# State products with stationary operands of 48 columns, the state added in two parts of 48 rows

## The chip, the cores and the metric

The kernel runs on one core of a Trainium2 chip. The core has five engines with a queue each: TensorE (PE in the profile; PEld is its loading of the stationary operand), VectorE (DVE), ScalarE (ACT), GpSimd (POOL) and SyncE (SP, which issues DMAs here). The metric is the device time of one execution in microseconds, the median of several runs. All arithmetic is fp32; on TensorE each product of fp32 operands shows as two passes, so each is two loads and two multiplications in the counts.

## What is computed

A linear attention with a state (the delta rule) over 4 batches, 8 heads, 768 steps and 48 columns per head, followed by a two-layer network with an exact GELU over the 3072 resulting rows:

```python
for t in range(S):                                   # S = 768, D = 48
    kt, vt, bt = k_n[:, :, t], v[:, :, t], beta[:, :, t, None]     # k_n: k over its norm
    y[:, :, t] = np.einsum('bhd,bhde->bhe', q[:, :, t], state)
    v_old = np.einsum('bhde,bhd->bhe', state, kt)
    state = state + bt[:, :, :, None] * np.einsum('bhd,bhe->bhde', kt, vt - v_old)
x = y.transpose(0, 2, 1, 3).reshape(B * S, H * D)    # 3072 x 384
h = x @ w_in                                         # 384 x 2048
out = (0.5 * h * (1.0 + erf(h / sqrt(2)))) @ w_out   # 2048 x 384
```

The state of each batch and head is a matrix of 48 x 48.

## The kernel before

The 768 steps are cut into NC = 12 chunks of C = 64. A unit is one chunk of a pair of batches (NA = 2 units per chunk, u.a = 0 and 1), so a unit's 128 rows are 64 steps of two batches. p (0 or 1) is the batch within the pair. The eight heads are written h = 2 j + r with j in 0..3 and r in 0 or 1.

Within a chunk the recurrence is solved at once: Gram matrices of the keys (`grams`, L368), an elimination on VectorE over 32 x 32 blocks (`eliminate_steps`, L443 and L445), two joins of blocks (`join_run`, L518), and then per chunk `state_steps`:

- `against_state` multiplies keys and queries with the state (L573) and forms W (L581, L582);
- `solve` makes U = Z W (L598), copied by ScalarE (L604);
- `outputs` calls `use` for both units: per unit 16 products with P, the masked query-key matrix (L616), into psY, and then `update`, 16 products of keys and U (L625), into psS. psY and psS are parts of one tile over two PSUM banks, hence both show as psY in the profile. For each unit there follow on VectorE `next_state` (L630), which adds psS to the state, and `read` (L639), four additions that make x, one row of the network's input per step;
- `turn` transposes x on TensorE (L660) into psX, and ScalarE copies it to xT (L661).

The state is a tile of 128 rows by unit, p, j and 48 columns: the rows of r = 0 begin at row 0, those of r = 1 at row 64. A head's state fills 48 of its 64 rows; in Kp, which holds the keys, the columns 48 to 63 of each head are zero (a memset at the start), and so rows 48 to 63 and 112 to 127 of psS and of the state are zero. Nothing reads those rows but the addition itself: `against_state` takes rows r * 64 to r * 64 + 47.

The network runs one chunk behind the attention: in stage c + 1 the chunk c goes through the first layer, 16 blocks of three products (`fc1`, L678) with a GELU on ScalarE (L680), and the second layer. From chunk 2 on the second layer is done in seven products of blocks in place of eight (`two`, L716), in the order n = 1, 5, 2, 6, 4, 7, 3. Products 6 and 7 use the same columns of the tile Y: 6 writes Y[:, 0], VectorE reads it (`read2`, L758), and 7 adds onto it (start is not set), is read by L761, and so on to L769. `mix` (L725 to L730) makes sums of G for these products on VectorE.

The order of work comes from `emit`, which sorts all steps by a time in units of stages. In the loop of stages only VectorE keeps the order in which the steps are emitted (`manual_schedule` with DVE alone); for the other engines a planner, which simulates the program with estimated costs, chooses the order within each queue. Chunk 0 and the start are emitted before the loop, in an order fixed for all engines, with `update` and `next_state` called for chunk 0 on their own. `update` and `next_state` are called for chunks 0 to 10: chunk 11 needs no further state.

"Stage w" below is the stretch in which state_steps(w) runs. In the profile the bursts of L625 begin at 58.0 us (chunk 0), 90.3 (1), 172.4 (2), 216.1 (3), 272.1 (4), 317.4 (5), 373.1 (6), 418.4 (7), 474.1 (8), 519.4 (9) and 572.8 (10).

Of the kernel before, what the change touches and what calls it, by code (L numbers as in the profile page):

```python
# [11 lines left out]
ALU = mybir.AluOpType  # L12
# [4 lines left out]
def kernel(  # L17
# [28 lines left out]
    nc = tc.nc  # L46
    B, H, S, D = q.shape
    DM, DF = moe_w_in.shape
    C = 64
# [8 lines left out]
    HALF = [slice(0, C), slice(C, 2 * C)]  # L58
# [40 lines left out]
    for c in range(NC):  # L99
        for a in range(NA):  # L100
            u = tiles[c, a] = Unit()
# [77 lines left out]
    St = cpool.tile([128, NA, 2, NP, D], F32)  # L179
# [426 lines left out]
    def use(us):  # L606

        for u in us:
            psY = dn("psY")
            u.psY = quarters(psY[:, :, 0:NP * D])  # L610
            u.psS = psY[:, :, NP * D:2 * NP * D].rearrange("q p (j d) -> q p j d", d=D)
            for k in range(NP // 2):
                for r in range(2):
                    for p, s in SIDES:
                        h = 4 * k + 2 * s + r
                        nc.tensor.matmul(u.psY[HALF[p ^ s], p, k, r, :], lhsT=u.P[HALF[p], h, :],  # L616
                                         rhs=u.U[HALF[p], h, :], start=True, stop=True)
            if u.c > 0:
                update(u)

    def update(u):
        if u.c < NC - 1:
            for j in range(NP):
                for r, p in QUADS:
                    nc.tensor.matmul(u.psS[HALF[r], p, j, :], lhsT=u.Kp[HALF[p], 2 * j + r, :],  # L625
                                     rhs=u.U[HALF[p], 2 * j + r, :], start=True, stop=True)

    def next_state(u):
        if u.c < NC - 1:
            nc.vector.tensor_tensor(St[:, u.a], St[:, u.a], u.psS, op=ALU.add)  # L630

    def read(u, copy=nc.scalar.copy):
        u.x = wk.tile([128, H, D], F32, tag="x", name="x")
# [7 lines left out]
    def outputs(us):  # L641
        use(us)
        for u in us:
            next_state(u)
            read(u)
# [252 lines left out]
    for u in first[:NA]:  # L898
        update(u)
# [4 lines left out]
    for u in first[:NA]:  # L904
        next_state(u)
# [44 lines left out]
    for w in range(3, NC):  # L950
# [6 lines left out]
        if w % 2:  # L957
            plan += [at(w + 0.09, w + 0.092, gram + query), at(w + 0.25, w + 0.95, state_steps(w))]
            if two_ahead:
                rows = eliminate_steps(w // 2 + 1)  # L960
# [45 lines left out]
```

## Time and profile before

| | us |
|---|---|
| median of 9 runs | 675.86 |
| lowest and highest | 674.47, 676.84 |
| the profiled execution | 675.02 |
| its span, first to last instruction | 673.3 |
| PE, DVE, ACT, POOL busy | 643.7, 452.3, 229.1, 82.1 |
| L625, 704 multiplications, busy | 14.9, 226 ns each |
| L625, 704 loads, busy | 13.1, 143 ns each |
| L630, 22 instructions, each (median) | 0.554 |
| L639, 80 instructions, each (median) | 0.356 |

Busy time of an engine counts overlapping instructions once. Small products on different quadrants of the array overlap, so their durations say little of the rate: what counts is the distance between starts. The mean granted TensorE clock is 0.98. In lines of the order of time the columns are start, duration of the merged group, engine, line, operation, written tile and read tiles, shape and count; in brackets stands how long the engine had been idle and what ended that.

### The profile page before, as it was taken

How to read it: one execution, taken by the hardware profiler on the slowest of the kernel's cores; microseconds unless marked ns; L12 is line 12 of the kernel's file. 1: busy time of each engine (PE TensorE's matmuls, PEld its weight loads, DVE VectorE, ACT ScalarE, POOL GpSimd, SP SyncE). 2: the span in 40 equal slices, each digit the busy share in tenths (PEclk: the TensorE clock that was granted, in tenths of full speed). 3: DMA queues.
4: the chain of work that ended last, by engine and by line, in shares of the span. 5: the costliest groups of instructions: out<-in, count | busy, mean ns of one | idle time of the engine just before them, and what ended most of it. 6: DMA issues, size and time to landing. Idle time of an engine off the chain costs nothing.

```text
span 673.3 us, 21703 instructions
## 1 busy us (share of the span) xinstructions
PE 643.7 (96%) x9542; PEld 561.4 (83%) x9542; DVE 452.3 (67%) x921; ACT 229.1 (34%) x605; POOL 82.1 (12%) x82
## 2 busy tenths in 40 slices
PE   6868998899899999999999999999999999999997
PEld 5666775676689989989989989989989989989996
DVE  6999999994689846479846479846479844324021
ACT  3457754614342143142143142143142132132220
POOL 4050300113111021111021111020111010000000
PEclk9966999999999999999999999999999999999999
DMA  8886565203432233511342511211301210100101
GB/s 124 187 245 171 114 177 130 47 1 65 84 45 34 52 46 51 82 31 27 57 53 44 85 27 27 52 21 31 67 3 26 55 17 3 25 1 2 24 1 25
DMA packets 158271, 39.76 MB, mean 59 GB/s; under 512 B 149984, under 2 KB 153056, under 8 KB 158176
## 3 DMA queue, kind: packets, MB, share of 16 engines
q1 hardware_dynamic: 152224, 33.26, 26.3%
q10 hardware_dynamic: 5952, 5.12, 3.3%
q8 instruction: 75, 1.23, 0.8%
q14 instruction: 20, 0.16, 0.1%
HBM read 33.62 MB, written 4.72 MB: 57 GB/s over the span
## 4 chain that ended last, share of the span: by engine, by line
PE 82%; DVE 10%; ACT 3%; issue 2%; DMA 2%; ACTq 0%; SPq 0%; DVEq 0%
PE psH L678 35%; PE psY L716 12%; PE psX L716 12%; PE psZ L716 4%; PE psK L573 3%; PE psJ L518 3%; PE psG L368 3%; PE psO L691 3%; PE psU L598 2%; PE psY L616 2%; DVE Nu L445 2%; DVE tmp L443 2%; DVE w_e L235 1%; DMA Kp<-in_k_dram 1%; PE psY L625 1%
## 5 line engine op out<-in xcount | busy, mean ns | idle before, releaser
L678 PE MATMUL psH<-xT,w_in_sb 128*128 128x256 f32 x1152 | 262.6, 384 | 4.1 <-ACT o_sb L695 2.3
L678 PEld LDWEIGHTS psH<-xT,w_in_sb 128*128 128x128 f32 x1152 | 216.0, 191 | 35.9 <-ACT o_sb L695 3.0
L680 ACT ACTIVATE G<-psH 128x256 f32<-128x256 f32 x192 | 73.6, 384 | 183.6 <-PE psH L678 171.6
L445 DVE TENSOR_TENSOR Nu<-Nu,tmp 128x30 f32<-128x30 f32 (+9 forms) x180 | 62.8, 349 | 6.2
L443 DVE TENSOR_TENSOR tmp<-Nu 128x30 f32<-128x30 f32 (+9 forms) x180 | 60.0, 333 | 5.1
L716 PE MATMUL psY<-w_out_sb,G 128*128 128x192 f32 x320 | 57.1, 330 | 1.1 <-DVE u L761 0.5
L716 PE MATMUL psX<-w_out_sb,G 128*128 128x192 f32 x320 | 56.2, 329 | 0.0
L716 PEld LDWEIGHTS psY<-w_out_sb,G 128*128 128x128 f32 x320 | 51.6, 190 | 3.1 <-DVE u L761 2.5
L716 PEld LDWEIGHTS psX<-w_out_sb,G 128*128 128x128 f32 x320 | 52.2, 190 | 0.7
L691 PE MATMUL psO<-w_out_sb,G 128*128 128x384 f32 x128 | 45.1, 495 | 1.6 <-DVE w_out_sb L236 1.6
L661 ACT COPY xT<-psX 128x384 f32<-128x384 f32 x24 | 11.4, 478 | 103.1 <-PE psX L660 102.0
L306 POOL TENSOR_TENSOR n<-n,half 128x16 f32<-128x16 f32 x10 | 29.4, 2939 | 88.8 <-DVE n L281 67.7
L691 PEld LDWEIGHTS psO<-w_out_sb,G 128*128 128x128 f32 x128 | 23.1, 190 | 16.9 <-DVE w_out_sb L236 4.0
L604 ACT COPY U<-psU 64x192 f32<-64x192 f32 x96 | 30.1, 313 | 19.6 <-PE psU L598 18.3
L403 DVE TENSOR_TENSOR P<-psG,mask 128x1024 f32<-128x1024 f32 x10 | 12.2, 1225 | 35.8 <-PE psG L368 35.8
L581 DVE TENSOR_TENSOR W<-psK,V 128x384 f32<-128x384 f32 x22 | 12.1, 551 | 29.1 <-ACT y L580 29.0
L725 DVE TENSOR_TENSOR S<-G 128x512 f32<-128x512 f32 x20 | 14.3, 714 | 25.8 <-ACT G L680 25.8
L467 POOL MEMSET Zf<- 32x512 f32 x23 | 12.4, 540 | 153.2 <-DVE Zf L458 152.2
L333 POOL TENSOR_TENSOR V<-V,n 128x384 f32<-128x384 f32 x18 | 17.1, 953 | 106.3 <-DMA V<-in_v_dram 57.7
L639 DVE TENSOR_TENSOR x<-psY,y 64x192 f32<-64x192 f32 x80 | 28.3, 354 | 0.9
L526 DVE TENSOR_TENSOR XM<-psJ,gm 32x512 f32<-32x512 f32 x20 | 13.8, 690 | 22.0 <-PE psJ L518 21.8
L716 PE MATMUL psY<-T,G 128*128 128x192 f32 x160 | 28.2, 329 | 0.0
(135 smaller groups left out, 878.4 us busy)
## 6 DMA issues: line engine op xcount, KB each, us to landing
Kp<-in_k_dram SPq DMA_DIRECT2D x76, 96.0 KB, 3.4
w_out_sb<-in_moe_w_in_dram SPq DMA_DIRECT2D x24, 256.0 KB, 4.2
V<-in_v_dram SPq DMA_DIRECT2D x48, 96.0 KB, 3.1
out_dram<-o_sb ACTq DMA_DIRECT2D x48, 96.0 KB, 2.2
w_raw<-in_moe_w_out_dram SPq DMA_DIRECT2D x10, 384.0 KB, 4.6
Zf<-in_moe_w_out_dram SPq DMA_DIRECT2D x6, 384.0 KB, 4.7
Qp<-in_q_dram SPq DMA_DIRECT2D x64, 32.0 KB, 2.2
Qp<-in_q_dram SPq DMA_DIRECT2D x16, 96.0 KB, 4.2
```

The source lines that it names most:

```text
L306: nc.gpsimd.tensor_tensor(flat, flat, half, op=ALU.pow)
L368: nc.tensor.matmul(psG[HALF[p], r, i * NP + j, :], lhsT=u.Kt[rows, p, j, :], rhs=(u.Qt if x else u.Kt)[rows, p, j, :], start=True, stop=True)
L443: nc.vector.tensor_tensor(tmp, nu[:, j + 1:, j:j + 1].to_broadcast([128, n, j]), nu[:, j:j + 1, 0:j].to_broadcast([128, n, j]), op=ALU.mult)
L445: nc.vector.tensor_tensor(nu[:, j + 1:, 0:j], nu[:, j + 1:, 0:j], tmp, op=ALU.add)
L518: nc.tensor.matmul(psJ[to, i, :], lhsT=(xm if level else off)[rows, u, :], rhs=zf[rows, u, HB:C] if level else xm[rows, u, :], start=True, ...
L573: nc.tensor.matmul(u.psK[to, x, r, j, :], lhsT=(u.Qt if x else u.Kt)[rows, p, j, :], rhs=St[rows, u.a, p, j, :], start=True, stop=True)
L604: copy(pairs(u.U[HALF[p]], s), u.psU[HALF[p ^ s], p])
L639: nc.vector.tensor_tensor(dst, src, pairs(u.y[HALF[p ^ s]], s), op=ALU.add)
L678: nc.tensor.matmul(psH, lhsT=w_in_sb[:, f // 2, m, f % 2 * 128:(f % 2 + 1) * 128], rhs=xTs[c][:, m, :], start=(m == 0), stop=(m == NM - 1))
L680: nc.scalar.activation(G[:, f, :], psH, ACT.Gelu)
L691: nc.tensor.matmul(u.psO, lhsT=G[:, f, u.a * 128:(u.a + 1) * 128], rhs=w_out_sb[:, f, :], start=(f == 0), stop=(f == NF - 1))
L716: nc.tensor.matmul(ps_, lhsT=lhs[:, f, :], rhs=rhs[:, f, :], start=first and f == 0, stop=f == FH - 1, skip_group_check=not first)
```

## The change

For chunks 2 to 10 the products of `update` take only the first 48 columns of each head's keys as the stationary operand, in place of 64 with the zero columns, and so write 48 rows of psS per r. The rows 48 to 63 and 112 to 127 of psS are then not written in those chunks, and `next_state` adds in two instructions, rows 0 to 47 and rows 64 to 111. Chunks 0 and 1 stay as they were.

```diff
@@ -622,12 +622,15 @@
         if u.c < NC - 1:
             for j in range(NP):
                 for r, p in QUADS:
-                    nc.tensor.matmul(u.psS[HALF[r], p, j, :], lhsT=u.Kp[HALF[p], 2 * j + r, :],
+                    m = C if u.c < 2 else D
+                    nc.tensor.matmul(u.psS[r * C:r * C + m, p, j, :],
+                                     lhsT=u.Kp[HALF[p], 2 * j + r, 0:m],
                                      rhs=u.U[HALF[p], 2 * j + r, :], start=True, stop=True)
 
     def next_state(u):
         if u.c < NC - 1:
-            nc.vector.tensor_tensor(St[:, u.a], St[:, u.a], u.psS, op=ALU.add)
+            for rows in [slice(0, 128)] if u.c < 2 else [slice(r * C, r * C + D) for r in range(2)]:
+                nc.vector.tensor_tensor(St[rows, u.a], St[rows, u.a], u.psS[rows], op=ALU.add)
```

## The prediction

> **What bounds the kernel now.** I read the page's first lines, then the table of stretches, then the order of time around the changed lines. The page:
>
> ```profile
> span 673.3 us, 21703 instructions
> ...
> PE 643.7 (96%) x9542; PEld 561.4 (83%) x9542; DVE 452.3 (67%) x921; ACT 229.1 (34%) x605; POOL 82.1 (12%) x82
> ...
> PE 82%; DVE 10%; ACT 3%; issue 2%; DMA 2%; ACTq 0%; SPq 0%; DVEq 0%
> ```
>
> TensorE (PE) is busy for 96% of the span and holds 82% of the chain that ended last. The table of stretches over two stages of the middle (stretch, its length, then the busy time of each engine) says how hard the bound is there:
>
> ```profile
> 260.00:310.00 50.00, 50.00 (x733) 45.62 (x732) 35.38 (x79) 15.78 (x40) 8.66 (x6) 1.00 0.35 57
> 310.00:361.00 51.00, 50.88 (x851) 46.08 (x850) 34.06 (x72) 15.37 (x37) 4.97 (x5) 1.00 0.26 41
> ```
>
> PE has no gap in them at a granted clock of 1.00, while VectorE (DVE) is busy for 34 to 35 of some 50 us. So time taken off PE's queue shortens these stages, and time put on DVE costs only where PE stands waiting for it. The question is how much room DVE has just behind the state sum. The order of time of stage 5 (start, us, engine, line, tiles, count):
>
> ```profile
> 318.31 0.56 PEld L625 LDWEIGHTS psY<-U,Kp 64*64 64x64 f32 x32
> ...
> 319.14 0.55 DVE L630 TENSOR_TENSOR St<-St,psY 128x384 f32<-128x384 f32 x1
> 319.61 1.45 DVE L639 TENSOR_TENSOR x<-psY,y 64x192 f32<-64x192 f32 x4
> 321.09 0.55 DVE L630 TENSOR_TENSOR St<-St,psY 128x384 f32<-128x384 f32 x1
> ...
> 321.56 1.46 DVE L639 TENSOR_TENSOR x<-psY,y 64x192 f32<-64x192 f32 x4
> ...
> 323.05 0.36 DVE L758 TENSOR_TENSOR u<-psY,p 128x192 f32<-128x192 f32 x1
> ...
> 324.08 0.41 PEld L660 LDWEIGHTS psX<-ident,x 128*128 128x128 f32 x3
> ...
> 324.46 2.58 PEld L716 LDWEIGHTS psY<-w_out_sb,G 128*128 128x128 f32 x16
> ```
>
> DVE works through sum, read, sum, read, L758 in one piece. The product at 324.46 (n = 7) adds onto the psY columns that L758 reads, so it may not begin before L758 is done, at 323.41: 1.05 us of room. Stages 7 and 9 repeat this to 0.01 us. Stage 3 has none left:
>
> ```profile
> 223.01 0.36 DVE L758 TENSOR_TENSOR u<-psY,p 128x192 f32<-128x192 f32 x1
> ...
> 223.42 2.57 PEld L716 LDWEIGHTS psY<-w_out_sb,G 128*128 128x128 f32 x16 [0.26 <-DVE u L758]
> ```
>
> There PE already stands 0.26 us for L758, and starts 0.05 us after its end (223.37).
>
> **What the change adds and removes.** It touches c = 2 to 10 with two units each: 18 bursts of L625 (of 22) and 18 sums of L630. No wait, tile, DMA or order by hand is changed.
>
> *PE.* A burst has 16 products in two passes, 32 pairs of load and multiplication. From the starts of the single records they come in groups of four quadrants, one group per 58 ns, so 8 x 58 = 0.465 us, which is also the distance from the burst before (L616 at 317.85) to the one at 318.31 above. What sets the 58? L368 streams 64 columns over a 64-column operand, L573 and L625 stream 48 over 64: all three take 58. So the streamed width does not decide up to 64, and the stationary width may. The trace has no operand of 48 columns. Bounds: 58 ns (L625 itself) and 33 ns per group of four, of L419, whose operands have 32 columns (and stream 32). Linear between them 48 gives 45.5, which I take: 12.5 x 8 = 0.10 us less per burst, 0.20 per stage, 18 x 0.10 = 1.8 us in all; by the ends 0 and 3.6.
>
> The Trainium skill speaks against a gain: "TensorEngine Tiling (Array Packing)", section Instruction Overhead, says that each product carries some 60 cycles whatever its free size and that nothing is won by cutting a dimension that is already small. The row differs, at 33 against 58 ns. By the rule PE would give nothing, by the row 1.8 us.
>
> *DVE.* Each sum of 128 rows, 0.55 us (median 0.554), becomes two of 48 rows with the same 384 columns. Does a sum of fewer rows take less? L526 with 32 rows x 512 takes 0.69 us, L725 with 128 rows x 512 takes 0.71: the columns count. So 18 instructions of 0.55 are added. Their distance is not their duration: before, L639 starts 0.47 after L630, that is 0.08 inside it; the four L639, which alternate between rows 0 and 64, are 0.365 apart with 0.356 each, with no overlap. The new second sum begins on row 64 and the L639 behind it on row 0, so I take them without overlap: 0.56 + 0.56 against 0.47, or +0.66 us per unit and +1.3 per stage. If they overlapped as L630 and L639 do now, it would be +0.47 and +0.9.
>
> The skill's page "VectorE: DVE Perf Modes", section Two Vector instructions with no wait between them, says that an instruction starts only after all earlier ones if its first row's quadrant differs from that of the last reader or writer of the same memory. It would make both new borders full ones: +1.3 per stage rather than +0.9.
>
> *Where it lands.* Stages 5, 7, 9: DVE was held by L730 before the bursts, so its train does not move up with PE. L758 ends at 323.41 + 1.3 = 324.7, the product starts at 324.8 instead of 324.46: +0.3 each, with PE's 0.2 swallowed, together +1.0. Stage 3: 223.37 + 1.3, so +1.3 whole. Stages 4, 6, 8, 10: L758 comes before the bursts, and what follows the reads has cover:
>
> ```profile
> 276.79 1.01 DVE L281 TENSOR_REDUCE n<-ksq 128x8 f32<-128x384 f32 x2
> ...
> 279.19 0.36 DVE L761 TENSOR_TENSOR u<-psY,p 128x192 f32<-128x192 f32 x1 [1.39 <-PE psY L716]
> ```
>
> DVE stands 1.39 us before L761 for PE; the 1.3 goes in there, and the turns (278.83 and 280.05) come over 3 us after their x is read (274.82 and 276.78). PE keeps its gain: 4 x -0.2 = -0.8. With that cover gone each would cost up to 1.3. Stage 2:
>
> ```profile
> 175.57 1.46 DVE L639 TENSOR_TENSOR x<-psY,y 64x192 f32<-64x192 f32 x4
> ...
> 176.86 0.52 ACT L278 ACTIVATE ksq<-Kp 128x384 f32<-128x384 f32 x1 [5.23 <-issue]
> ...
> 177.29 0.46 ACT L661 COPY xT<-psX 128x384 f32<-128x384 f32 x1
> ...
> 177.80 0.31 PEld L660 LDWEIGHTS psX<-ident,x 128*128 128x128 f32 x3 [0.81 <-ACT xT L661]
> ```
>
> L278 waits, by the semaphores of its record, for a DMA into Kp (the page of waits can only say "issue") and holds ScalarE's queue, so unit 0's later x is hidden behind it. Unit 1's x ends at 177.03 + 1.3 - 0.1 (the first sum starts earlier by one shorter burst) = 178.2, and its turn then waits for that: +0.5 against 177.80, and with it the xT that the next stage begins with.
>
> Sum: 0.5 + 1.3 + 1.0 - 0.8 = +2.0 us, on the profiled execution's 675.02 (span 673.3 and 1.7 around it) 677.0. That execution lies 0.84 below the median of the nine, so I add to the median: 675.86 + 2.0 = **677.9 us**, 0.3% slower.
>
> **Rivals.** *The adds overlap, and all cancels.* With +0.9 per stage stages 5, 7, 9 end L758 at 324.3, where PE, 0.2 earlier, wants it at 324.26: about -0.1 each; stage 3 +0.9, stage 2 +0.1, the even ones -0.8: 0.0, so 675.9. For it: L639 starts inside L630 today. Against: the rows that alternate do not overlap.
>
> *PE's gain comes through whole, faster.* Only DVE's order is fixed by hand in the loop; PE's is laid out by a planner from estimated costs. If its estimate of a later L758 moves another ready piece (a gram, a turn) ahead of the product n = 7, the wait has work under it, and -1.8 remains: 674.0. It decides from the point where at least 1.3 us of PE work is ready in stage 3 and 0.5 in 5, 7 and 9. For it: in stage 4 eight products of L368 stand between turn and product, just where PE would wait for L761. Against: in odd stages the next turn needs the single psX buffer, and the next grams a Kt that DVE turns only at 230.37.
>
> *48 columns cost what 64 do.* Then the PE term is 0: stage 2 +0.6, stage 3 +1.3, odd ones +1.0, even ones 0, so +2.9, 678.8. For it: operands lie in quadrants of 64 x 64 all the same. Against: nothing between 33 and 58 ns is seen.
>
> **How the numbers follow.** Forecast 0.46, cancelled 0.24, PE's gain whole 0.22, no PE gain 0.08. Under and over 0.2% (1.35 us, about what a measurement of this kernel can tell from no change): faster takes the third case, 0.22; no change takes the second and the 0.06 of the forecast that a smaller distance on DVE brings under 1.35, 0.30; slower is the rest, 0.48. The forecast's own range runs from +0.8 (stage 2 hidden, the adds 1.15 per stage: stage 3 +1.15, the odd ones +0.15 each, the even ones -0.8) over +1.2 (loads of 48 columns at the price of 32: the even stages give 0.8 more) to +2.9 (at the price of 64). With the faster case the range is 674.0 to 679.0.
>
> **What would show it.** In the changed trace: L625's loads with 48 columns at a distance of about 0.36 us per burst (0.465 if the width does not count); two L630 per unit of 0.55 each, 0.56 apart and L639 0.56 behind; L716 in stages 3, 5, 7, 9 with idle time put down to L758 (1.5 us in stage 3, 0.5 in the others); DVE before L761 in stage 4 with almost no wait left. I am wrong if PE's order in odd stages has other work before product 7, if that idle time is absent, or if the even stages show PE waiting for L761 or L639.

## The result, and the profile after

| | before | after |
|---|---|---|
| median, us | 675.86 (31 runs, 674.28 to 677.07) | 678.94 (10 runs, 677.66 to 679.67) |
| ratio | | 1.0046, 95% interval 1.0037 to 1.0055 |
| span of the profiled execution | 673.3 | 677.2 |

The change makes the kernel slower by 3.1 us (by the interval 2.5 to 3.7). The forecast was +2.0 us. The page of the changed kernel, the same lines as before (line numbers behind L625 are moved by one to three: the products of `update` are L626, the sums L633, the reads L642, the turns L663, the second layer L719, `read2` L761 to L772):

```profile
span 677.2 us, 21722 instructions
...
PE 640.9 (95%) x9542; PEld 557.9 (82%) x9542; DVE 463.4 (68%) x939; ACT 229.1 (34%) x605; POOL 82.3 (12%) x82
...
PE 73%; DVE 19%; issue 3%; ACT 3%; DMA 1%; POOL 0%; ACTq 0%; DVEq 0%; POOLq 0%
```

PE works 2.8 us less and DVE 11.1 us more, with 18 instructions more. In the chain that ended last PE's share falls from 82 to 73% and DVE's rises from 10 to 19%. These 9 points are some 60 us of the span, far more than the 11 us that were added on DVE: the shares say over which engine the chain runs, not what the change costs.

The answer for L626 shows the products (engine, operation, tiles, count, shortest/median/longest ns, first and last start, forms as counted in every fourth record), and the order of time of PE's loads in stage 5 shows the bursts:

```profile
L626 PEld LDWEIGHTS psY<-U,Kp x704: 122/122/228, 57.5 to 578.1; 64*48 64x48 f32 x144, 64*64 64x64 f32 x32
L626 PE MATMUL psY<-U,Kp x704: 205/205/340, 57.5 to 578.1; 64*48 64x48 f32 x144, 64*64 64x48 f32 x32
```

```profile
320.74 0.46 PEld L626 LDWEIGHTS psY<-U,Kp 64*48 64x48 f32 x32
321.10 0.56 PEld L616 LDWEIGHTS psY<-U,P 64*64 64x64 f32 x32
```

From the narrow burst to the next one it is 0.36 us, where it was 0.465: the width of the stationary operand does count. In the records a group of four loads takes 45 ns, against 58 with 64 columns.

What DVE pays, and PE for it, in the order of time of stage 5, and below it of stage 3:

```profile
322.50 1.11 DVE L633 TENSOR_TENSOR St<-St,psY 48x384 f32<-48x384 f32 x2
323.63 1.46 DVE L642 TENSOR_TENSOR x<-psY,y 64x192 f32<-64x192 f32 x4
...
325.12 1.12 DVE L633 TENSOR_TENSOR St<-St,psY 48x384 f32<-48x384 f32 x2
326.25 1.46 DVE L642 TENSOR_TENSOR x<-psY,y 64x192 f32<-64x192 f32 x4
...
327.74 0.36 DVE L761 TENSOR_TENSOR u<-psY,p 128x192 f32<-128x192 f32 x1
...
328.15 2.57 PEld L719 LDWEIGHTS psY<-w_out_sb,G 128*128 128x128 f32 x16 [0.52 <-DVE u L761]
```

```profile
226.41 0.36 DVE L761 TENSOR_TENSOR u<-psY,p 128x192 f32<-128x192 f32 x1
...
226.83 2.57 PEld L719 LDWEIGHTS psY<-w_out_sb,G 128*128 128x128 f32 x16 [1.35 <-DVE u L761]
```

The two parts of a sum follow each other without overlap (1.11 for two), and the reads begin 1.13 after the first part, where they began 0.47 after the single sum: +0.66 per unit. Product 7 now stands for L761, 0.52 us in stage 5 and 1.35 in stage 3, where it stood 0 and 0.26.

To see where the 3 us come from, I laid the two traces side by side: for every run of multiplications of one line on PE, its start after minus its start before, each counted from the start of its own span. The difference is 0.77 us already at the first burst of stage 2 (L616). That part belongs to the start, ahead of any changed instruction; in the kernels below it lies between -0.1 and +1.7 at the same place, though every engine has the same instructions in the same order up to there, so it is a property of the execution. From there on it changes by:

| stage | 2 | 3 | 4 | 5 | 6 | 7 | 8 | 9 | 10 | sum |
|---|---|---|---|---|---|---|---|---|---|---|
| measured, us | +1.75 | +0.88 | -0.04 | +0.32 | -0.01 | +0.33 | -0.21 | +0.33 | -0.21 | +3.14 |
| forecast, us | +0.5 | +1.3 | -0.2 | +0.33 | -0.2 | +0.33 | -0.2 | +0.33 | -0.2 | +2.0 |

(Stage 2 is counted up to the first L573 of stage 3, stage 3 up to its product 7, stage 4 from there to the first L573 of stage 5, and each later stage to the first L573 of the next. The numbers that are read from traces below are counted in the same way.) The sum agrees with the +3.1 of the medians.

### The profile page after: what moved, and what is told of

Read it like the earlier page. It is cut to its first block, busy times and chain, and to the rows that moved or that the text cites. A ratio compares the mean times of both kernels' runs of the same rounds, so it can differ in the third digit from the quotient of the medians.

```text
span 677.2 us, 21722 instructions
## 1 busy us (share of the span) xinstructions
PE 640.9 (95%) x9542; PEld 557.9 (82%) x9542; DVE 463.4 (68%) x939; ACT 229.1 (34%) x605; POOL 82.3 (12%) x82
## 4 chain that ended last, share of the span: by engine, by line
PE 73%; DVE 19%; issue 3%; ACT 3%; DMA 1%; POOL 0%; ACTq 0%; DVEq 0%; POOLq 0%
PE psH L681 33%; PE psY L719 11%; PE psX L719 10%; PE psZ L719 3%; DVE Nu L445 3%; PE psJ L518 3%; PE psK L573 3%; PE psG L368 3%; DVE tmp L443 3%; PE psO L694 3%; DVE x L642 2%; PE psU L598 2%; DVE St L633 2%; DVE w_e L235 1%; DVE w_out_sb L236 1%
## 5 line engine op out<-in xcount | busy, mean ns | idle before, releaser
L719 PE MATMUL psY<-w_out_sb,G 128*128 128x192 f32 x320 | 57.4, 331 | 3.0 <-DVE u L761 1.9
L719 PEld LDWEIGHTS psY<-w_out_sb,G 128*128 128x128 f32 x320 | 51.6, 190 | 5.7 <-DVE u L761 2.9
L719 PE MATMUL psX<-w_out_sb,G 128*128 128x192 f32 x320 | 56.2, 329 | 0.0
L719 PEld LDWEIGHTS psX<-w_out_sb,G 128*128 128x128 f32 x320 | 52.2, 190 | 0.7
L633 DVE TENSOR_TENSOR St<-St,psY 48x384 f32<-48x384 f32 (+1 forms) x40 | 21.9, 551 | 11.2 <-PE psY L626 10.6
L642 DVE TENSOR_TENSOR x<-psY,y 64x192 f32<-64x192 f32 x80 | 28.4, 355 | 1.1
```

The costliest lines, as they stand in the source:

```text
L633: nc.vector.tensor_tensor(St[rows, u.a], St[rows, u.a], u.psS[rows], op=ALU.add)
L642: nc.vector.tensor_tensor(dst, src, pairs(u.y[HALF[p ^ s]], s), op=ALU.add)
L719: nc.tensor.matmul(ps_, lhsT=lhs[:, f, :], rhs=rhs[:, f, :], start=first and f == 0, stop=f == FH - 1, skip_group_check=not first)
```

## The experiments

Is it the sums at all? The first kernel has the two sums alone.

```diff
-            nc.vector.tensor_tensor(St[:, u.a], St[:, u.a], u.psS, op=ALU.add)
+            for rows in [slice(0, 128)] if u.c < 2 else [slice(r * C, r * C + D) for r in range(2)]:
+                nc.vector.tensor_tensor(St[rows, u.a], St[rows, u.a], u.psS[rows], op=ALU.add)
```

> The sums in two parts alone, with products of 64 columns as before. Theory (DVE's longer train, +1.3 us per stage, reaches PE in stages 2 and 3 whole and in 5, 7, 9 beyond 1.05 us of room, nothing in the even ones; PE's shorter bursts give 0.2 per stage where PE is not waiting): stages 2 and 3 together +2.7, stages 5, 7, 9 +0.33 each, even ones 0: +3.7 us against before, more than the whole change (+3.1). L761's idle time ahead of product 7 in stage 5 stays near 0.3 to 0.5 us. Rival (the loss comes from the narrow products or from the planner's other order on PE, not from the sums): within 1 us of before.

Measured: 680.36 against 675.57 us, ratio 1.0074 (1.0061 to 1.0088), +4.8 us. The sums are the loss, and the narrow products take about 1.7 of it back (4.8 less 3.1, out of two comparisons that are each sure to some 0.6 to 0.9 us); by the two traces it is 1.0 (4.14 less 3.14). The expected 3.7 lies just below the interval of 4.1 to 5.9. The trace places the loss: stage 2 +1.86, stage 3 +1.11, stages 5, 7 and 9 +0.33 each, stages 4 and 6 up to +0.1, stages 8 and 10 nothing. The opposite kernel, narrow products with the sums as they were, was not tried: one sum over both halves would read rows that nothing has written in that chunk.

The second has the whole change in the even stages alone, the third in chunks 2 and 3 alone.

```diff
-                    m = C if u.c < 2 else D
+                    m = D if u.c in (4, 6, 8, 10) else C
...
-            for rows in [slice(0, 128)] if u.c < 2 else [slice(r * C, r * C + D) for r in range(2)]:
+            for rows in [slice(0, 128)] if u.c not in (4, 6, 8, 10) else [slice(r * C, r * C + D) for r in range(2)]:
```

> The whole change for chunks 4, 6, 8 and 10 alone; the others as before. Theory: DVE has over 1.3 us of waiting for PE in these stages, so only PE's gain is left, 4 times -0.2, less some 0.1 in stages where the turn waits for the copy of psX: -0.4 to -0.8 us against before. Rival (each added sum costs its time wherever it stands): +1.3 per stage less 0.2, +4.4 us. Rival (PE gains nothing anywhere): 0 to +0.4.

Measured: 674.80 against 675.57, ratio 0.9991 (0.9980 to 1.0002). The interval rules out +4.4 us, but not zero; its trace shows PE 0.44 us earlier at the end of stage 10 than at the Gram products ahead of stage 3, at the low end of what was expected: 0.21 is kept in each of stages 8 and 10, while in 4 and 6 the same 0.21 is lost again. Where it goes is seen in stage 4 of the changed kernel, with the same turn of the kernel before below it, which stood for nothing:

```profile
281.38 1.01 DVE L281 TENSOR_REDUCE n<-ksq 128x8 f32<-128x384 f32 x2
...
282.02 0.98 ACT L278 ACTIVATE ksq<-Kp 128x384 f32<-128x384 f32 x2 [9.59 <-issue]
...
282.91 0.46 ACT L664 COPY xT<-psX 128x384 f32<-128x384 f32 x1
...
283.42 0.31 PEld L663 LDWEIGHTS psX<-ident,x 128*128 128x128 f32 x3 [0.28 <-ACT xT L664]
```

```profile
280.05 0.32 PEld L660 LDWEIGHTS psX<-ident,x 128*128 128x128 f32 x3
```

The sums push L281, and the two L278 that refill ksq run right behind it; ScalarE is then busy with them when the copy of xT comes up, and unit 1's turn waits for the single psX buffer. DVE's room was there, as forecast; the room in ScalarE's queue was not looked at.

```diff
-                    m = C if u.c < 2 else D
+                    m = D if u.c in (2, 3) else C
```

(and the same condition in `next_state`.)

> The whole change for chunks 2 and 3 alone. Theory: from the reads of stage 2 to L761 of stage 3 DVE and PE wait for each other in one chain, and DVE's +1.3 counts in both: +2.5 to +2.8 us against before, nearly all of the whole change's +3.1. Rival (my prediction's working: stage 2 +0.5, stage 3 +1.3): +1.8. Rival (spread evenly over the nine chunks): +0.7.

Measured: 678.51 against 675.57, ratio 1.0043 (1.0029 to 1.0057), +2.9 us. Two of nine chunks carry nearly the whole loss; an even spread is ruled out, and the prediction's own 1.8 lies just below the interval (2.0 to 3.9). By the trace stage 2 costs +1.75 and stage 3 +0.90.

The next one takes chunk 2 out.

```diff
-                    m = C if u.c < 2 else D
+                    m = C if u.c < 3 else D
```

(and the same bound in `next_state`.)

> The whole change from chunk 3 on; chunk 2 as before. Theory (the chunk's part in stage 2 costs some 1.3 us because DVE's train runs on from the reads through the sums of weights to Kt, for which PE's Gram products wait): +3.1 less 1.3, +1.6 to +1.9 us against before. Rival (stage 2 costs 0.5, as the prediction had it, and the rest lies in later stages): +2.6.

Measured: 677.73 against 676.03, ratio 1.0032 (1.0022 to 1.0042), +1.7 us by the medians; the interval (1.5 to 2.8) would still hold the rival's 2.6. The trace decides: without chunk 2 the difference at product 7 of stage 3 is +1.32 above that at the end of stage 2, the forecast's +1.3. So stage 3 alone costs 1.3, and the 0.9 seen with chunk 2 in is smaller because PE came into stage 3 late already. Stage 2 is the term that was mis-sized.

Why, is read in stage 2, first of the kernel before, then of the one with chunks 2 and 3 changed:

```profile
178.38 0.48 ACT L661 COPY xT<-psX 128x384 f32<-128x384 f32 x1 [0.25 <-PE psX L660]
178.44 1.12 ACTq L685 DMA_DIRECT2D out_dram<-o_sb  x2
...
178.91 3.75 PEld L678 LDWEIGHTS psH<-xT,w_in_sb 128*128 128x128 f32 x18 [0.81 <-ACT xT L661]
...
183.23 0.30 PEld L678 LDWEIGHTS psH<-xT,w_in_sb 128*128 128x128 f32 x2
...
184.94 0.21 PEld L368 LDWEIGHTS psG<-Kt 48*64 48x64 f32 x8 [1.40 <-DVE Kt L353]
```

```profile
177.97 1.28 ACTq L688 DMA_DIRECT2D out_dram<-o_sb  x2
...
178.27 0.31 PEld L663 LDWEIGHTS psX<-ident,x 128*128 128x128 f32 x3 [1.46 <-ACT o_sb L698]
...
179.29 0.48 ACT L664 COPY xT<-psX 128x384 f32<-128x384 f32 x1 [1.35 <-PE psX L663]
...
179.82 3.75 PEld L681 LDWEIGHTS psH<-xT,w_in_sb 128*128 128x128 f32 x18 [1.24 <-ACT xT L664]
...
185.31 1.30 DVE L353 STREAM_TRANSPOSE Kt<-Kb 128x512 f32<-128x512 f32 x2
...
186.07 0.43 PEld L368 LDWEIGHTS psG<-Kt 48*64 48x64 f32 x20 [1.89 <-DVE Kt L353]
```

Unit 1's turn starts 0.47 later than before (178.27 against 177.80), as forecast. (The second trace is 0.10 ahead of the first at the first burst of the stage; counted from there, this delay and those that follow are 0.1 larger.) But the planner has now put the issue of the two output DMAs ahead of the copy of xT in ScalarE's queue; they hold it until 179.25, and the first layer begins 0.91 later (179.82 against 178.91). And DVE's train does not end with the reads: `finish`, three sums of weights and the turned Kt (L353) follow without a gap, and the Gram products wait 1.89 us for Kt, where they waited 1.40. Ahead of that wait PE had two passes of the first layer to do before (183.23, 2 x 0.215 us); in the new order they stand behind it. PE's waits from 172 to 199 us (who for whom, us in total, times, longest), before and with chunks 2 and 3 changed:

```profile
PE psG L368 <- DVE Kt L353: 1.0, 1, 1.0
PE psH L678 <- ACT xT L661: 0.6, 1, 0.6
PE psX L660 <- DVE x L639: 0.3, 1, 0.3
PE psX L660 <- ACT xT L661: 0.2, 1, 0.2
```

```profile
PE psG L368 <- DVE Kt L353: 1.7, 1, 1.7
PE psX L663 <- DVE x L642: 1.3, 2, 0.9
PE psH L681 <- ACT xT L664: 1.0, 1, 1.0
```

They grow by 1.9 us: 0.8 at the turns, 0.4 at the first layer and 0.7 at the Gram products. The two narrow bursts give 0.2 of it back.

My theory by then was that the late Kt alone is what stage 2 costs. The next kernel puts it to the test: chunk 2 alone, with both reads ahead of all four sums.

```diff
         for u in us:
-            next_state(u)
+            if u.c != 2:
+                next_state(u)
             read(u)
+        if us[0].c == 2:
+            for u in us:
+                next_state(u)
```

> The change for chunk 2 alone, and there the reads of both units stand ahead of all four sums on DVE, so x is ready 0.5 to 1.5 us earlier than before, while the sums of weights and Kt behind them stay as late as in the whole change. Theory (DVE's train to Kt is what stage 2 pays by): the turns no longer wait for x, the Gram products still wait about 2 us or more for Kt, and PE reaches the state products of stage 3 (L573) 1.2 to 1.9 us later than in before, counted from the first burst of stage 2. Rival (the later x and its turn are what is paid, as the prediction had it): 0.2 us later or earlier.

```profile
178.42 0.48 ACT L668 COPY xT<-psX 128x384 f32<-128x384 f32 x1 [0.26 <-PE psX L667]
178.48 1.18 ACTq L692 DMA_DIRECT2D out_dram<-o_sb  x2
...
178.94 1.16 PEld L685 LDWEIGHTS psH<-xT,w_in_sb 128*128 128x128 f32 x6 [0.81 <-ACT xT L668]
```

```profile
183.26 0.73 PEld L685 LDWEIGHTS psH<-xT,w_in_sb 128*128 128x128 f32 x4
...
184.60 0.30 PEld L685 LDWEIGHTS psH<-xT,w_in_sb 128*128 128x128 f32 x2
...
185.36 1.30 DVE L353 STREAM_TRANSPOSE Kt<-Kb 128x512 f32<-128x512 f32 x2
...
186.12 1.15 PEld L368 LDWEIGHTS psG<-Kt 48*64 48x64 f32 x64 [1.22 <-DVE Kt L353]
```

The theory fell. Kt is just as late (185.36 against 185.31), and yet PE reaches L573 of stage 3 0.23 us earlier than before, counted from the first burst of stage 2. With x early the copy stands ahead of the DMAs again, the first layer begins at 178.94, and the planner lays six of its passes, where there were two, in front of the Gram products, which shortens their wait. The delay of DVE is not gone: it comes out at product 7 of stage 3, where the difference rises by 0.89 though chunk 3 is unchanged; from stage 2 to the end this kernel loses 0.77. So stage 2's loss on PE came from the later x, through the order in ScalarE's queue and the order on PE that went with it. PE's waits above say where the time stands; what the order of each queue would cost by itself was not tried. One profiled execution stands behind this (675.69 against 676.15 us), so its time is not compared.

The last three ask for a better version. In the first, chunk 2 is as before, and the odd chunks' sums come behind the turns.

```diff
+    def late_sum(u):
+        return u.c > 2 and u.c % 2 == 1
...
-            next_state(u)
+            if not late_sum(u):
+                next_state(u)
             read(u)
...
+        return steps + [(0.01, next_state, u) for u in us if late_sum(u)]
```

> Products of 48 columns and two sums from chunk 3 on, chunk 2 as before, and in odd chunks the sums of both units moved behind the turns, so behind L761 and L764 and ahead of the last product's read. Theory: in odd stages DVE's train ahead of product 7 is then shorter than before by two sums (0.9 us), PE waits for nothing there and keeps its 0.2 (in stage 3 also the 0.26 of waiting that was there before); even stages -0.2 each: -1.3 to -1.9 us against before, faster. Rival (the added sums cost DVE time that PE pays later in the stage, or the later release of the psY tile holds up the next stage's products): 0 to +3.

Measured: 676.84 against 675.57, ratio 1.0018 (1.0006 to 1.0030), slower: the expectation failed. Product 7 waits for nothing any more, but a new wait has come, in every odd stage (here stage 3):

```profile
228.56 2.24 DVE L633 TENSOR_TENSOR St<-St,psY 48x384 f32<-48x384 f32 x4
...
231.39 0.36 DVE L777 TENSOR_TENSOR o_sb<-psY,u 128x192 f32<-128x192 f32 x1
...
231.80 7.64 PEld L686 LDWEIGHTS psH<-xT,w_in_sb 128*128 128x128 f32 x36 [0.75 <-DVE o_sb L777]
```

The four sums stand ahead of the last product's read, L777, which frees the PSUM buffer that the next stage's first layer needs. From stage to stage PE loses 0.62 us by it. So the sums go behind that read, with 48 columns and, to tell the two gains apart, with 64 columns and one sum per unit:

```diff
-            next_state(u)
+            if u.c < 3 or u.c % 2 == 0:
+                next_state(u)
...
+    plan += [at(c + 0.985, c + 0.99, [(1.0, next_state, tiles[c, a]) for a in range(NA)])
+             for c in range(3, NC, 2)]
```

> Products of 48 columns and two sums from chunk 3 on, chunk 2 as before, and in the odd chunks the sums of both units moved to the end of the stage, behind the last product's read, which frees the buffer that the next stage's first layer waits for. Theory: the 0.62 us per odd stage that the run with sums behind the turns lost at that read is gone; PE keeps 0.2 per stage and loses the 0.2 of waiting in stage 3: -1.3 to -1.7 us against before, faster. Rival (any added DVE time in these stages ends up on PE, at the joins or the Gram products): 0 or slower.

> Only the move of the odd chunks' sums to the end of the stage, with products of 64 columns and one sum per unit as before. Theory: only the waiting in stage 3 goes (0.2 to 0.3 us), the rest of before has room there: -0.1 to -0.4 us against before, and 1.2 us or more slower than the run with the same order and 48 columns. Rival (the move brings the gain, the narrow products nothing): equal to that run.

Measured, on the same chip against 676.03: with 48 columns 674.44, ratio 0.9976 (0.9964 to 0.9988), 1.6 us faster than before and so some 4.7 faster than the change as given (1.6 and 3.1; the two were not run side by side); with 64 columns 675.64, ratio 0.9996 (0.9986 to 1.0005). So the narrow products are worth about 1.2 us once the sums are out of the way, and the move by itself little.

```profile
330.07 0.36 DVE L773 TENSOR_TENSOR o_sb<-psY,u 128x192 f32<-128x192 f32 x1 [1.00 <-PE psY L720]
330.34 2.24 DVE L633 TENSOR_TENSOR St<-St,psY 48x384 f32<-48x384 f32 x4
```

In stage 5 the four sums now run behind L773, for which DVE had stood 1.00 us; nothing on PE waits for them. In its trace PE gains 0.55 us over stages 3 and 4, where the wait for product 7 is gone, 0.21 in each of stages 5 and 7 to 10, and nothing in 6: 1.62 in all.

The last kernel asks whether half the gain can be had without a second sum: 64 columns for r = 0 and 48 for r = 1, so that rows 0 to 111 are written whole and one sum of 112 rows does.

```diff
-                    m = C if u.c < 2 else D
+                    m = C if u.c < 2 or r == 0 else D
...
+            rows = slice(0, 128 if u.c < 2 else C + D)
+            nc.vector.tensor_tensor(St[rows, u.a], St[rows, u.a], u.psS[rows], op=ALU.add)
```

> From chunk 2 on the products into the upper rows keep 64 columns and those into the lower rows take 48, so rows 0 to 111 are written without a gap and one sum of 112 rows does it: no instruction is added on DVE. Theory A (each quadrant of the array loads by itself, and a group of four goes at the pace of the widest): 58 ns per group as before, nothing gained. Theory B (the loads share one path, or a quadrant's lag is carried over to the next group): 45 to 55 ns per group, 0.36 to 0.44 us per burst.

By its trace (it has one execution) nothing is gained: from the start of the two units' four bursts to the next product it is 2.01 us in stage 5, as before (316.92 to 318.93), and the traces lie within 0.1 us of each other through all stages. The narrow loads run ahead of the wide ones, out of step with them, and the widest sets the end (theory A).

## Why the prediction was right or wrong

- *PE's term* (0.10 us per burst by a line between 33 and 58 ns, 0.20 per stage, 1.8 in all): right. Measured are 45 ns per group, where 45.5 was taken, 0.36 us per narrow burst, and 0.21 us in the undisturbed stages 8 and 10. The page's rule weighed against it, no gain from a small dimension made smaller, gives its example for the free size of a product; for the columns of the stationary operand it did not hold here: 45 against 58 ns.
- *DVE's term* (two sums of 0.55 without overlap, +0.66 per unit): right to 0.01 us, so the rival of overlapping adds is out. It agrees with the rule of the Trainium skill's page "VectorE: DVE Perf Modes", section Two Vector instructions with no wait between them: the sum that starts on row 64 and the read behind it on row 0 each start only when the one before has ended (the second sum 0.55 us after the first in stage 5, the read 0.57 after the second).
- *Stages 5, 7, 9* (+0.33 each): +0.32, +0.33, +0.33, through the wait that was named. *Stage 3* (+1.3): +1.32 with chunk 3 as the first one changed, but 0.88 in the change itself, because PE comes late out of stage 2. That these 0.4 were put too high hid a part of what stage 2 was put too low, which is luck.
- *Even stages* (-0.2 each): right in 8 and 10 (-0.21); in 4 and 6 (-0.04 and -0.01) the gain was lost in ScalarE's queue.
- *Stage 2* (+0.5): this is the step that failed: 1.75, so 1.25 us too low, more than the whole distance between forecast and result. It followed the later x to its turn and its xT and stopped there ("its turn then waits for that: +0.5"). The turn was later by that much. What was late next was not asked: ScalarE's queue and PE's, which the planner orders anew when x comes later, and the Gram products, which waited 0.7 longer.
- *The rival of a planner that helps* named stages 3, 5, 7 and 9; there product 7 waits bare (1.35 and 0.52 us), and no other work was moved ahead of it. The order did change in stage 2, of which the rival did not speak, and there it added to the loss. Only when the reads stood ahead of the sums did it lay work into the wait.

## What to carry to other kernels

An edit that shortens the bound engine by lengthening another is decided where the bound engine waits for the other next; list those places stage by stage, because two of nine carried over four fifths of the loss here. Move the added work behind the last instruction that someone waits for (here the read that frees a buffer), not merely behind the first: some 4.7 us lay between the change as given and the same change with its sums in the right place and chunk 2 left alone. And where a planner orders the other queues, a step that comes later can be followed only as far as its own wait; the order behind it has to be seen again.

## What the runs showed of the hardware

Loads of an fp32 stationary operand that go to four quadrants of the array in turn cost by their columns, also between the sizes of the tiles: a group of four repeats every 33 ns with 32 columns (L419 of the kernel before, streaming 32, in the second half of its burst, where the loads run evenly), 45 with 48 (L626, streaming 48) and 58 with 64 (L625 streaming 48, L368 streaming 64). With 64 columns in two quadrants and 48 in the other two the pair of units took the 2.01 us of 64 everywhere. And the issue of two DMAs on ScalarE's queue, 1.28 us in one group, delayed the copy that stood behind it in the kernel with chunks 2 and 3 changed: the turn had ended at 178.82, the issue ended at 179.25, and the copy began at 179.29.
